# A decode kernel's TensorE program as loops of two units with fixed addresses: K turned into one of two slots, V landing in one of two, w_o between the loops

## The chip, the cores and the metric

The kernel runs on one core of one Trainium2 chip. The metric is device time in microseconds (us). Five engines work side by side, each from its own program: TensorE (PE), VectorE (DVE), ScalarE (ACT), GpSimd (POOL) and SyncE (SP), which here only issues transfers. Sixteen DMA engines carry the transfers.

## The reference, cut to what matters

Two layers of attention over a cache and a small feed-forward network, for 4 rows of 512 numbers, each layer run with the same weights and the same caches:

```python
for layer in range(2):
    x = x + attention(layernorm(x), k_cache, v_cache, wq, wo)
    x = x + (silu(n @ w_gate) * (n @ w_up)) @ w_down      # n = layernorm(x)
# attention: q = n @ wq, 32 heads; head h of row b reads group h // 4:
#   p = softmax(q . k_cache[b, g] / sqrt(128)), o = p @ v_cache[b, g], then o @ wo
# k_cache, v_cache: (4, 8, 8192, 128) bf16
```

There are 4 x 8 = 32 pairs of row and group. A pair is called a unit; it needs one K block and one V block of 8192 x 128 bf16, 2 MB each.

## The kernel before, in words

**Slots.** SBUF holds eight slots of 2 MB (`kv`, L157 to L158). `pump` (L316) walks one list of loads (`items`, L279 to L284) in order and issues the next whenever a slot fits: any free slot will do for any K or V, except that the last loads ahead of the feed-forward weights use slots 0 to 5 alone. The order of a layer is K0 K1 V0 K2 V1 K3 V2 ... and at its end w_gate, w_up and w_down, which take slots 6 and 7 and a piece behind them. Layer 1 starts with units 29, 30, 31, whose K and V are kept in six slots from layer 0 (L267 to L278); then come units 0 to 28. While they are worked through, V of unit 0 and K of unit 2 come in by halves over K of units 29 and 30 (`halves`, L288 and `half`, L350).

**One unit.** DVE turns K in place, in eight pieces q of 1024 keys (`turn`, L396, a 32 x 32 block transpose, L401). For each piece TensorE runs four score matmuls (`scores`, L414, L421) into one of two PSUM banks, so 32 a unit. The left-hand matrix `zq` holds the unit's queries between zeros; POOL writes it for each unit (L412). Then come the softmax steps: a maximum over the free axis (L427), a transpose (L431), a maximum of it (L434), a copy (L437), a spread by matmul (L443), exp on ACT (L449), a transpose on DVE (L454), the sum (L457, L459). For V, sixteen matmuls (`block`, L517) use the transposed p; ACT and DVE pick out and add the diagonal blocks (L526, L531), a matmul adds rows (L536), and DVE scales into `oT` (L556). The last two units of a layer do V in 64 small matmuls (L549). Once the four units of a group are done, `out_proj` (L575) multiplies by that group's part of w_o: 16 matmuls at L581, a DVE copy at L584, 16 matmuls at L587, and an addition to x.

**Order.** The program of every engine is written out flat. `keys` (L473) and `values` (L496) put blocks into a list with an estimated time each; `drain` (L467) emits them so that DVE's turning runs 2.0 us of estimated time ahead of TensorE; `advance` and `flush` (L382, L389) put the softmax steps (`line`) and the steps after V (`after`) between the blocks. TensorE takes V of unit u right after the scores of unit u+1: K0, K1, V0, K2, V1, K3, V2 and so on. `_Sync` (L21) keeps a count for each engine and puts in the waits. `finished` (L363) frees a slot behind the last matmul that reads it, and calls `pump`.

**Feed-forward.** `ffn` (L647) uses slots 6 and 7 for weights; at its end (L683) these two are free again, and K of units 0 and 1 of the next layer are loaded into them.

Of the kernel before, what the change touches and what calls it, by code (L numbers as in the profile page):

```python
# [6 lines left out]
ALU = mybir.AluOpType  # L7
# [13 lines left out]
class _Sync:  # L21

    def __init__(self, engines, prog_sems):
        self.eng = engines
        self.prog = prog_sems
        self.count = {n: 0 for n in engines}
        self.waited = {}
        self.res = {}
        self.semval = {}

# [24 lines left out]
    def _wait(self, engname, need):  # L55
        e = self.eng[engname]
        for sem, val in need:
            k = (engname, id(sem))
            if self.waited.get(k, 0) >= val:
                continue  # L60
            if sem is self.prog.get(engname) and (val > self.count[engname] or engname == "pe"):
                continue
            e.wait_ge(sem, val)
            self.waited[k] = val

    def _record(self, engname, sv, reads, writes):
# [6 lines left out]
        for r in reads:  # L73
            rec = self.res.get(r)
            if rec is None:
                rec = self.res[r] = _Rec()
            rec.r[engname] = sv

# [25 lines left out]
def bass_interleave_layers__gqa_block_cached__swiglu_ffn__decode_kernel(  # L104
# [43 lines left out]
    with ExitStack() as es:  # L148
# [7 lines left out]
        o4 = sb("o4", [P, REP, B], BF16)  # L156
# [24 lines left out]
        xs = sb("xs", [P, B], FP32)  # L181
        vs = sb("vs", [P, B], FP32)
        lnv = sb("lnv", [P, B], FP32)
        rstd = sb("rstd", [P, B], FP32)
        oT = sb("oT", [P, 2, REP, B], BF16)
# [4 lines left out]
        zq = sb("zq", [P, 4, ZP + P], BF16)  # L190
# [99 lines left out]
        free = list(range(NSLOT))  # L290
        slot_of = {}

# [23 lines left out]
        def pump():  # L316
            while issued[0] < len(items):
                n = issued[0]
                it = items[n]
                if it[0][0] == "w":  # L320
                    if it[0] == "wg":
                        if not {NKEEP, NKEEP + 1} <= set(free):
                            return
                        free[:] = [s for s in free if s < NKEEP]
                    load_weight(*it)
                    issued[0] += 1
                    continue

                late = any(e - 10 < n < e for e in ends)
                fit = [s for s in free if s < NKEEP or not late]  # L330
                if not fit:
                    return
                s = fit[0] if late else max(fit, key=lambda s: s >= NKEEP)
# [29 lines left out]
        def finished(it):  # L363
            kind, L, u = it
            if (kind, 1, u) in kept and L == 0:
                slot_of[kind, 1, u] = slot_of[it]
                if kind == "K":
                    turned.update((1, u, q) for q in range(NB))
            elif it in halves:
                half(it, 1)  # L370
                pump()
            else:
                free.append(slot_of[it])
# [22 lines left out]
        def turn(L, u, q):  # L396


            s = slot_of["K", L, u]
            w = kv[:, s, q * TB * Dh:(q + 1) * TB * Dh].bitcast(FP32)  # L400
            T.op("dve", lambda e: e.transpose(w, w), reads=[f"s{s}.{q}"], writes=[f"s{s}.{q}"])  # L401
            turned.add((L, u, q))

        def place_q(u, eng="pool", src=qr, keys_=SCR):
# [4 lines left out]
            dst = zq[:, :, ZP:].rearrange("p c (a x) -> p c a x", a=NA)[:, :, :, 0:REP]  # L409
# [4 lines left out]
        def scores(L, u, q):  # L414

            s = slot_of["K", L, u]
# [3 lines left out]
            for c in range(4):  # L420
                T.op("pe", lambda e: e.matmul(bank(bk)[:, 0:SW], lhsT=zq[:, c, z0:z0 + P], rhs=w[:, :, c // 2, :, c % 2],  # L421
                                              start=(q == 0 and c == 0), stop=(q == NB - 1 and c == 3)),
                     reads=[f"s{s}.{q}", "zq"], writes=[f"pb{bk}"], sig=(c == 3))
# [6 lines left out]
        def max_t(u):  # L430
            T.op("pe", lambda e: e.matmul(bank(STEP)[0:1, 0:P], lhsT=mx[:], rhs=identf[:], is_transpose=True,  # L431
                                          start=True, stop=True),
                 reads=["mx", "ident"], writes=[f"pb{STEP}"])
# [7 lines left out]
        def exps(u):  # L441
            bk = SBK[turn_of[u]]
            T.op("pe", lambda e: e.matmul(bank(STEP)[:, 0:1], lhsT=mrow,  # L443
                                          rhs=onesf[0:1, :], start=True, stop=True),
                 reads=["pb", "onesf"], writes=[f"pb{STEP}"])
# [10 lines left out]
        def total(u):  # L456
            T.op("pe", lambda e: e.matmul(bank(TOT)[:, 0:REP], lhsT=ones, rhs=rsm[:], start=True, stop=True),  # L457
                 reads=["rsm", "onesf"], writes=[f"pb{TOT}"])
# [4 lines left out]

        blocks = []
# [8 lines left out]
        def keys(L, u):  # L473
            def block(q):
                first = u == unit_order[L][0]
                if q == 0 and not first:
# [6 lines left out]
                if q == NB - 1:  # L483
                    finished(("K", L, u))
# [8 lines left out]

        done = set()

        def values(L, u):  # L496
            g, b = unit_gb(u)
            bk = OBK[turn_of[u]]

# [8 lines left out]
            def block(i):  # L508
# [5 lines left out]
                for t in range(TB):  # L514
                    j = t % NA
                    c0 = t * QB + i * NV * REP
                    T.op("pe", lambda e: e.matmul(bank(bk)[j * QB:j * QB + NV * REP, :],  # L517
                                                  lhsT=pT[:, turn_of[u], c0:c0 + NV * REP], rhs=v[:, t, NV * i:NV * (i + 1), :],
                                                  start=(i == 0 and t == j), stop=(i == 1 and t >= TB - NA)),
                         reads=[f"s{s}.{NV * i + k}" for k in range(NV)] + [f"pT{turn_of[u]}"], writes=[f"pb{bk}"],  # L520
                         sig=(t == TB - 1))
# [13 lines left out]
            def add_rows():  # L535
                T.op("pe", lambda e: e.matmul(bank(LNB)[:, 0:REP], lhsT=acc[:], rhs=head[:], start=True, stop=True),  # L536
                     reads=["acc", "head"], writes=[f"pb{LNB}"])
                scale_o(LNB)

            def block_last(q):  # L540
# [6 lines left out]
                for t in range(q * TB, (q + 1) * TB):  # L547
                    c0 = (t % TB) * QB + REP * q
                    T.op("pe", lambda e: e.matmul(bank(bk)[:, 0:REP], lhsT=kv[:, s, t * Dh:(t + 1) * Dh],  # L549
                                                  rhs=pT[:, turn_of[u], c0:c0 + REP], start=(t == 0), stop=(t == TT - 1)),  # L550
                         reads=[f"s{s}.{q}", f"pT{turn_of[u]}"], writes=[f"pb{bk}"], sig=(t % TB == TB - 1))
# [3 lines left out]
            def scale_o(k):  # L555
                T.op("dve", lambda e: e.tensor_tensor(oT[:, g // (G - 1), :, b], bank(k)[:, 0:REP], rl[:, rl_of[u], :],  # L556
                                                      ALU.mult),
                     reads=[f"pb{k}", f"rl{rl_of[u]}"], writes=[f"oT{g // (G - 1)}"])
# [8 lines left out]
            if all((L, g * B + k) in done for k in range(B)):  # L567
                rest.append([0.5, None, lambda: out_proj(g)])
# [6 lines left out]
        def out_proj(g):  # L575

            pick = ident.rearrange("p (j e) -> p e j", e=REP)
            ob = bank(OUTB)[:, XB:2 * XB].rearrange("p (e b) -> p e b", b=B)
            for c in range(REP):
                for h in range(REP):  # L580
                    T.op("pe", lambda e: e.matmul(ob[h * QB:(h + 1) * QB, c, :], lhsT=pick[:, c, :],  # L581
                                                  rhs=oT[:, g // (G - 1), h, :], start=True, stop=True),
                         reads=[f"oT{g // (G - 1)}", "ident"], writes=[f"pb{OUTB}"], sig=(h == REP - 1))
            T.op("dve", lambda e: e.tensor_copy(o4[:], ob), reads=[f"pb{OUTB}"], writes=["o4"])  # L584
            for nt in range(KT):
                for c in range(REP):
                    T.op("pe", lambda e: e.matmul(bank(OUTB)[:, nt * B:(nt + 1) * B],  # L587
                                                  lhsT=wo_sb[:, g, c, nt * P:(nt + 1) * P], rhs=o4[:, c, :],
                                                  start=(c == 0), stop=(c == REP - 1)),
                         reads=[f"wo{g // (G // 4)}", "o4"], writes=[f"pb{OUTB}"], sig=(c == REP - 1))  # L590
# [6 lines left out]
        def center():  # L597
            T.op("dve", lambda e: e.tensor_reduce(xs[:], xT[:].rearrange("p (k b) -> p b k", b=B), AX.X, ALU.add),
                 reads=["x"], writes=["xs"])
            T.op("pe", lambda e: e.matmul(bank(LNB)[:, 0:B], lhsT=ones, rhs=xs[:], start=True, stop=True),  # L600
                 reads=["xs", "onesf"], writes=[f"pb{LNB}"])
# [11 lines left out]
        def deviation(bias, bkey):  # L613
            T.op("pe", lambda e: e.matmul(bank(TOT)[:, 0:B], lhsT=ones, rhs=vs[:], start=True, stop=True),
                 reads=["vs", "onesf"], writes=[f"pb{TOT}"])
            T.op("act", lambda e: e.activation(lnv[:], bank(TOT)[:, 0:B], ACTF.Ln, scale=1.0 / D, bias=eps_sb[:]),
                 reads=[f"pb{TOT}", "eps"], writes=["lnv"])
            T.op("act", lambda e: e.activation(rstd[:], lnv[:], ACTF.Exp, scale=-0.5, bias=bias[:]),
                 reads=["lnv", bkey], writes=["rstd"])

        def qproj(gs, u=None):
            h0, nh = gs[0] * REP, len(gs) * REP
            for h in range(h0, h0 + nh):
                for kt in range(KT):
                    T.op("pe", lambda e: e.matmul(bank(LNB)[:, h * B:(h + 1) * B],  # L625
                                                  lhsT=wq_sb[:, kt, h * Dh:(h + 1) * Dh],
                                                  rhs=xn[:, kt * B:(kt + 1) * B],
                                                  start=(kt == 0), stop=(kt == KT - 1)),
# [7 lines left out]
            for c in range(4):  # L636
                for a in range(NA):
                    T.op("pe", lambda e: e.matmul(ob[a * QB:(a + 1) * QB, c, :, h0:h0 + nh],
                                                  lhsT=pick[:, c // 2, :, c % 2],
                                                  rhs=qT[:, :, h0:h0 + nh], start=True, stop=True),  # L640
# [120 lines left out]
```

## Time and profile before

| what | value |
|---|---|
| median of 3 runs | 654.95 us (654.82 to 656.93) |
| the profiled execution: its time | 655.51 us |
| its span, first to last instruction | 653.7 us |
| TensorE matmul busy | 500.5 us, 77% |
| DVE busy | 446.1 us, 68% |
| ACT, POOL busy | 18%, 3% |
| moved by DMA | 274.64 MB, 420 GB/s over the span |
| K loads: median from issue to landing | 30.0 us |
| V loads: median from issue to landing | 33.8 us |
| granted TensorE clock | 0.824 |

The page cuts the span into 40 slices of 16.3 us, and gives for each the busy share of each engine, the granted TensorE clock, the share of the DMA engines and the rate. It lists the DMA queues by kind: `hardware_dynamic` is the data, `instruction` is the fetching of programs (queue 8 in 16 KB packets, 38 of them; queue 14 in smaller ones). The trace keeps each DMA packet with its start and length, and for each load sixteen increments of its semaphore, one from each DMA engine, with their times: the first and the last tell when the earliest and the latest engine had its share of a load done.

### The profile page before, as it was taken

The numbers are of one execution on the slowest core, as the hardware profiler recorded it, in microseconds if no ns is written. First come the engines' busy times: TensorE is split into PE (matmuls) and PEld (weight loads), VectorE is DVE, ScalarE is ACT, GpSimd is POOL, SyncE is SP. The second block draws the span as 40 slices with busy tenths as digits, with TensorE's granted clock in tenths as the row PEclk, the third lists the DMA queues.
The fourth block names the chain that finished last, engine by engine and source line by source line (L and its number), as shares of the span: only waits on it lengthen the run. The fifth ranks groups of instructions, "written<-read, shape, count | busy, mean of one in ns | idle before, by whom it ended". The sixth has DMA issues, their size and how long they took to land.

```text
span 653.7 us, 11807 instructions
## 1 busy us (share of the span) xinstructions
PE 500.5 (77%) x4896; PEld 319.2 (49%) x4896; DVE 446.1 (68%) x1079; ACT 116.4 (18%) x391; POOL 19.3 (3%) x73
## 2 busy tenths in 40 slices
PE   1766787977777877787876988887688787786886
PEld 1544444544444544544555655554354454443456
DVE  2556676776776777776752399996677677676682
ACT  0021121221221221221220212221122122121120
POOL 0000000000000000000000000000000000000000
PEclk9897788777978778789685989997978887797895
DMA  9999999999999999999999999999999999999996
GB/s 368 428 425 423 438 429 427 432 431 429 430 431 429 430 430 432 430 432 428 427 416 375 398 411 431 430 428 429 430 428 429 433 430 430 432 427 429 432 420 239
DMA packets 24085, 274.64 MB, mean 420 GB/s; under 512 B 2392, under 2 KB 2400, under 8 KB 7904
## 3 DMA queue, kind: packets, MB, share of 16 engines
q1 hardware_dynamic: 24032, 273.89, 98.9%
q8 instruction: 38, 0.62, 0.3%
q14 instruction: 15, 0.12, 0.0%
HBM read 273.88 MB, written 0.00 MB: 419 GB/s over the span
## 4 chain that ended last, share of the span: by engine, by line
DMA 66%; DVE 17%; PE 13%; SPq 3%; issue 1%; ACT 0%; POOL 0%; DVEq 0%; POOLq 0%
DMA kvf<-in_A_k_cache_dram 63%; DVE kvf L401 11%; PE ps L421 8%; DVE acc L531 3%; DMA kvf<-in_B_w_down_dram 3%; SPq L93 2%; PE ps L517 1%; DVE one L427 1%; DVE pT L454 1%; PE ps L587 1%; DVE m L434 1%; PE ps L625 1%; PE ps L457 0%; PE ps L676 0%; PE ps L549 0%
## 5 line engine op out<-in xcount | busy, mean ns | idle before, releaser
L401 DVE STREAM_TRANSPOSE kvf<-kvf 128x512 f32<-128x512 f32 x488 | 322.4, 686 | 121.8 <-DMA kvf<-in_A_k_cache_dram 121.8
L421 PE MATMUL ps<-kvf,zq 128*128 128x256 bf16 x2048 | 346.2, 314 | 18.2 <-DVE kvf L401 15.7
L421 PEld LDWEIGHTS ps<-kvf,zq 128*128 128x128 bf16 x2048 | 211.3, 115 | 89.8 <-DVE kvf L401 40.4
L437 ACT ACTIVATE pb<-m 1x128 f32<-1x128 f32 x64 | 19.7, 308 | 453.5 <-DVE m L434 453.5
L431 PE MATMUL ps<-identf,one 128*1 128x128 f32 x64 | 18.3, 286 | 68.3 <-DVE one L427 68.3
L517 PE MATMUL ps<-kvf,pT 128*16 128x512 bf16 x960 | 68.5, 409 | 0.9 <-DVE rl L459 0.9
L531 DVE SCALAR_TENSOR_TENSOR acc<-ps,own,acc 128x128 f32<-128x128 f32 x180 | 63.1, 351 | 6.5 <-ACT acc L526 1.9
L431 PEld LDWEIGHTS ps<-identf,one 128*1 128x1 f32 x64 | 5.1, 80 | 99.4 <-DVE one L427 93.2
L536 PE MATMUL ps<-head,acc 128*128 128x4 f32 x120 | 26.4, 290 | 17.9 <-DVE acc L531 17.7
L536 PEld LDWEIGHTS ps<-head,acc 128*128 128x128 f32 x120 | 22.8, 237 | 34.2 <-DVE acc L531 33.6
L443 PE MATMUL ps<-one,pb 1*128 1x1 f32 x128 | 27.8, 284 | 14.1 <-ACT pb L437 13.8
L443 PEld LDWEIGHTS ps<-one,pb 1*128 1x128 f32 x128 | 22.4, 217 | 32.8 <-ACT pb L437 29.1
L449 ACT ACTIVATE pb<-ps,one,rstd 128x256 bf16<-128x256 f32 x64 | 36.2, 565 | 2.1
L412 POOL TENSOR_TENSOR zq<-scr,quad 128x64 bf16<-128x64 bf16 x62 | 18.2, 293 | 608.1 <-PE ps L421 569.4
L517 PEld LDWEIGHTS ps<-kvf,pT 128*16 128x16 bf16 x960 | 19.3, 91 | 32.8 <-issue 21.2
L427 DVE TENSOR_REDUCE one<-ps 128x1 f32<-128x256 f32 x64 | 25.6, 399 | 13.1 <-PE ps L421 12.7
L454 DVE STREAM_TRANSPOSE pT<-pb 128x256 bf16<-128x256 bf16 x64 | 25.9, 405 | 1.9 <-ACT pb L449 1.9
L457 PEld LDWEIGHTS ps<-rsm,one 128*128 128x128 f32 x128 | 24.5, 237 | 3.0 <-ACT rsm L451 0.9
L457 PE MATMUL ps<-rsm,one 128*128 128x4 f32 x128 | 21.6, 239 | 0.0
L447 ACT ACTIVATE one<-ps,rstd 128x1 f32<-128x1 f32 x64 | 16.7, 261 | 25.8 <-PE ps L443 25.8
L526 ACT ACTIVATE acc<-ps,own 128x128 f32<-128x128 f32 x60 | 20.6, 343 | 0.0
L434 DVE TENSOR_REDUCE m<-ps 1x4 f32<-1x128 f32 x64 | 15.6, 244 | 6.5 <-PE ps L431 6.5
(66 smaller groups left out, 165.9 us busy)
## 6 DMA issues: line engine op xcount, KB each, us to landing
kvf<-in_A_k_cache_dram SPq DMA_DIRECT2D x60, 2048.0 KB, 30.0
kvf<-in_A_v_cache_dram SPq DMA_DIRECT2D x58, 2048.0 KB, 33.8
wq_sb<-in_A_wq_dram SPq DMA_DIRECT2D x4, 1024.0 KB, 7.6
wo_sb<-in_A_wo_dram SPq DMA_DIRECT2D x4, 1024.0 KB, 34.5
kvf<-in_A_v_cache_dram SPq DMA_DIRECT2D x8, 512.0 KB, 19.3
kvf<-in_B_w_gate_dram SPq DMA_DIRECT2D x2, 1792.0 KB, 23.2
kvf<-in_B_w_down_dram SPq DMA_DIRECT2D x4, 768.0 KB, 16.0
kvf<-in_A_v_cache_dram SPq DMA_DIRECT2D x2, 1024.0 KB, 7.0
```

The costliest lines, as they stand in the source:

```text
L401: T.op("dve", lambda e: e.transpose(w, w), reads=[f"s{s}.{q}"], writes=[f"s{s}.{q}"])
L421: T.op("pe", lambda e: e.matmul(bank(bk)[:, 0:SW], lhsT=zq[:, c, z0:z0 + P], rhs=w[:, :, c // 2, :, c % 2], start=(q == 0 and c == 0), sto ...
L427: T.op("dve", lambda e: e.tensor_reduce(mx[:], bank(bk)[:, 0:SW], AX.X, ALU.max), reads=[f"pb{bk}"], writes=["mx"])
L431: T.op("pe", lambda e: e.matmul(bank(STEP)[0:1, 0:P], lhsT=mx[:], rhs=identf[:], is_transpose=True, start=True, stop=True), reads=["mx", " ...
L434: T.op("dve", lambda e: e.tensor_reduce(m4[:], bank(STEP)[0:1, 0:P].rearrange("p (x h) -> p h x", h=REP), AX.X, ALU.max, negate=True), rea ...
L443: T.op("pe", lambda e: e.matmul(bank(STEP)[:, 0:1], lhsT=mrow, rhs=onesf[0:1, :], start=True, stop=True), reads=["pb", "onesf"], writes=[f ...
L449: T.op("act", lambda e: e.activation(pb[:], bank(bk)[:, 0:SW], ACTF.Exp, bias=nm[:], scale=by, accum_out=rs[:]), reads=[f"pb{bk}", "nm", " ...
L454: T.op("dve", lambda e: e.transpose(pT[:, turn_of[u], :], pb[:]), reads=["pb"], writes=[f"pT{turn_of[u]}"])
L457: T.op("pe", lambda e: e.matmul(bank(TOT)[:, 0:REP], lhsT=ones, rhs=rsm[:], start=True, stop=True), reads=["rsm", "onesf"], writes=[f"pb{T ...
L517: T.op("pe", lambda e: e.matmul(bank(bk)[j * QB:j * QB + NV * REP, :], lhsT=pT[:, turn_of[u], c0:c0 + NV * REP], rhs=v[:, t, NV * i:NV * ( ...
L531: T.op("dve", lambda e: e.scalar_tensor_tensor(acc[:], bank(bk)[:, k * Dh:(k + 1) * Dh], own[:, k:k + 1], acc[:], op0=ALU.mult, op1=ALU.ad ...
L536: T.op("pe", lambda e: e.matmul(bank(LNB)[:, 0:REP], lhsT=acc[:], rhs=head[:], start=True, stop=True), reads=["acc", "head"], writes=[f"pb ...
```

## The change

**Slots have fixed uses.** For most units K lands in slot 0 to 3 (by u - 2, modulo 4) and DVE's turning writes it into slot 6 or 7 (by u modulo 2), where TensorE reads it; the landing slot is free once it is turned out. V lands in slot 4 or 5 (by u modulo 2). Units 0 and 1 land in 6 and 7 and are turned in place, and the units 29 to 31 and the last two of a layer are turned in place where they landed. `pump` still goes through the same list in order, but each load now has one slot, and the list waits for that one.

**TensorE's program is recorded first** (`T.pe` puts each matmul with its waits on a tape) and emitted at the end by `roll`. It looks for stretches in which unit n and unit n + 2 have the same instructions, addresses and semaphores, and the awaited values grow by a constant. Each such stretch of at least three repeats becomes a loop on TensorE of two units; at the head of each turn the awaited values are worked out in registers from the loop's counter. The loop's head is placed at the start of a fetch block. The other engines' programs stay flat.

**w_o.** `project` takes several groups at once, at four places between loops: at unit 14 and 26 of layer 0 (groups 0 to 2 and 3 to 5) and at positions 17 and 27 of layer 1 (groups 0 to 2 and 3, 4), with the copy on ACT; the other groups as before. `oT` has a place for each group.

Some small tensors share a place (`xs` and `lnv` become `vs`), and `zq` keeps one run of zeros instead of four.

```diff
-        free = list(range(NSLOT))
+        free = set(range(NSLOT))
+        NLAND = NSLOT - 4
+        scored = set()
+        def home(it):
+            kind, L, u = it
+            if kind == "K" and u < 2:
+                return NKEEP + u
+            if kind == "K" or it in split:
+                return (u - (2 if kind == "K" else 1)) % NLAND
+            return NLAND + u % 2
+        def turned_in(L, u):
+            if u < 2 or u >= NU - NRES or u in unit_order[L][-2:]:
+                return slot_of["K", L, u]
+            return NKEEP + u % 2
...
-                late = any(e - 10 < n < e for e in ends)
-                fit = [s for s in free if s < NKEEP or not late]
-                if not fit:
+                s = home(it)
+                if s not in free:
                     return
...
-            T.op("dve", lambda e: e.transpose(w, w), reads=[f"s{s}.{q}"], writes=[f"s{s}.{q}"])
+            T.op("dve", lambda e: e.transpose(dst, src), reads=[f"s{s}.{q}"], writes=[f"s{to}.{q}"])
             turned.add((L, u, q))
+            if q == NB - 1 and to != s:
+                free.add(s)
+                pump()
...
+        between = {(0, 14): [0, 1, 2], (0, 26): [3, 4, 5], (1, 17): [0, 1, 2], (1, 27): [3, 4]}
...
+        def roll():
+            ops = T.tape
+            part = [ops[a:b] for a, b in zip(heads, tails[1:] + [len(ops)])]
+            said = [[(repr(aps), [id(w[0]) for w in left], sig, kw) for aps, left, sig, kw in seg] for seg in part]
...
+            stops = [n for n in range(1, len(heads)) if heads[n] != tails[n] or n == NU] + [len(heads)]
...
+                    while m + 2 < stop and said[m] == said[m + 2] and strides(m) and strides(m) == strides(n + (m - n) % 2):
+                        m += 1
...
+                if turns < 3:
+                    continue
...
+                with nc.Fori(1, 1 + turns, 1, engines=(pe,), head_slot={pe: 0}) as i:
+                    value = {}
+                    for _, left, _, _ in body:
+                        for sem_, v in left:
+                            d, = step[id(sem_)]
+                            value[id(sem_), v] = nc.tensor.to_reg(i * d + (v - d))
+                    T.play(body, lambda sem_, v: value[id(sem_), v])
```

## The prediction

> **What bounds the kernel now.** I began with the slices of the page.
>
> ```profile
> PE   1766787977777877787876988887688787786886
> DVE  2556676776776777776752399996677677676682
> ```
>
> The slices of the transfers are steadier:
>
> ```profile
> DMA  9999999999999999999999999999999999999996
> GB/s 368 428 425 423 438 429 427 432 431 429 430 431 429 430 430 432 430 432 428 427 416 375 398 411 431 430 428 429 430 428 429 433 430 430 432 427 429 432 420 239
> ```
>
> The transfers run at 427 to 433 GB/s nearly all the time, and no engine is full except DVE in slices 24 to 27 (376 to 441 us). So the kernel ends when its bytes have been moved. There is one dip, slices 21 to 24 (327 to 392 us), between the layers.
>
> Next I read the queues.
>
> ```profile
> q1 hardware_dynamic: 24032, 273.89, 98.9%
> q8 instruction: 38, 0.62, 0.3%
> ```
>
> Queue 8 is TensorE's program: 38 packets of 16 KB. On average that is 0.3%, but a load is done only when the slowest of the 16 engines has done its share. In the packet records a data packet of 16 KB takes 611 ns; a fetch takes 879 to 968 ns and the data packet behind it 1.08 to 1.16 us, so each fetch holds up its DMA engine by 1.41 us. The lengths repeat with a period of eight (934, 932, 924, 967, 961, 954, 879, 878, then 942, 933, 924 ...), and where the packets can be followed one to the next, fetches eight apart lie on one engine: eight engines take turns, the other eight get none. The landing times show it: the first K has its first share at 17.3 and its last at 17.9 us, 0.6 apart; by 31.5 us the two are 1.9 apart, by 196 us 3.3, by 334 us 3.8. In the stages where the queue never runs dry it grows with fetches 1, 9, 25 and 33 (28, 181, 428 and 580 us). At the end it is 4.9 us (first engine 644.9, last 649.9).
>
> Then the chain of waits, for the dip:
>
> ```profile
> 333.72 17.27 DMA kvf<-in_B_w_down_dram
> 351.04 1.08 PE ps L676 x32
> 355.17 1.04 PE ps L421 x4
> ...
> 398.64 1.21 DVE kvf L401 x2
> ...
> 411.66 0.63 PE ps L421 x4
> 412.35 21.91 DMA kvf<-in_A_k_cache_dram
> ```
>
> From 352 to 412 us the chain is TensorE and DVE: six slots were kept, so little could be loaded ahead, and computation is behind. Last, the timeline of SP, with TensorE's V matmuls:
>
> ```profile
> 366.70 0.33 SPq L93 DMA_DIRECT2D kvf<-in_A_v_cache_dram  x1
> 371.77 0.33 SPq L93 DMA_DIRECT2D kvf<-in_A_k_cache_dram  x1
> 372.75 0.33 SPq L93 DMA_DIRECT2D kvf<-in_A_v_cache_dram  x1
> 384.17 0.33 SPq L93 DMA_DIRECT2D kvf<-in_A_k_cache_dram  x1
> 385.15 0.33 SPq L93 DMA_DIRECT2D kvf<-in_A_v_cache_dram  x1
> 398.11 1.04 PE L517 MATMUL ps<-kvf,pT 128*16 128x512 bf16 x16
> 399.24 0.36 SPq L93 DMA_DIRECT2D kvf<-in_A_v_cache_dram  x1
> ```
>
> These are layer 1's V1 (366.70), K3, V2, K4 (384.17) and V3 (385.15, in the slot that V31 left). V1 is worked through at 398.11 to 399.15, 20 us after it landed (378.9), and its slot is reloaded at 399.24.
>
> **The change, part by part.**
>
> *Fixed V slots: a new wait.* V3 may go into slot 5 alone, and slot 5 holds V1 until 399.2. SP's list is in order, so K5, V4 and all later loads queue behind V3. K4 (slot 2, free when V31 is done, 385.2) is then the last load under way; it lands first at about 392. From an idle queue, layer 1's K0 took from 349.02 to its first share at 355.88, 6.86 us, of which 4.87 is the load itself (the step from landing to landing); so 2.0 us pass ahead of the first byte. V3 lands first at 399.24 + 2.0 + 4.87 = 406.1 instead of 396.58: +9.5 us on an engine without fetches. Such an engine then goes without a gap to the end in both kernels (396.58 to 644.92 before), so this is never made up. Computation is not starved by it: V3 is needed at 412, K5 lands at 411.0 where DVE reaches it at 411.6; K6, at 420.7, is 1.2 late, and from there the transfers bound again.
>
> *The same wait elsewhere.* In steady state V u is done 4 to 8 us after landing, while K, V and K (14.6 us) are in the queue ahead of the load that needs its slot; less 2.0 that leaves some 5 us. The tightest are 242.72 + 2.0 against 246.1, when the earliest engine wants it, 1.4 us, and ahead of w_gate V30, which goes at 320.8 instead of 306.2 and is wanted at 323.9: 1.1 us. At the kernel's start V2 could go at 38.6 and is wanted at 46.6. I cost these at nothing; the cover is these margins, and where one is gone, each us over it is a us of the whole. K's four landing slots are freed by DVE, earlier than before, and slots 6 and 7 are rewritten a whole unit after TensorE read them: nothing.
>
> *Turning into another slot* (L401, 656 to 712 ns a piece in place): the trace shows no out-of-place one of this shape. Between -0.5 and +0.5 us for eight pieces, by that row's own width; one unit (K2) lies ahead of V1's end. I take 0.
>
> *The loop.* By the positions given for w_o, the stretches are 0 to 13, 14 to 25, 26 to 31, 32 to 48, 49 to 58 and 59 to 63, and six units at least must repeat: about 2 to 13, 14 to 25, 37 to 48 (ahead of it V0 and K0, K1 lie elsewhere) and 50 to 58, so some 44 of 64 units. A unit has 110 records of matmuls and weight loads (32 + 16 + 1 + 2 + 2 + 2 pairs), and fetches lie 250 records apart. Not streamed: 44 x 110 = 4840, less four bodies of some 270, less up to a block of padding for each: 12 to 13 blocks, so about 25 fetches instead of 38. By 350 us there were 19 and will be some 13: the engine hit most had three (1, 9, 17) and gets two, -1.4 us for the end of layer 0 and with it V1's end. After 401 us come about 10 instead of 15. The idle gap lets the engines start together, 0.6 to 1.3 apart (17.9 and 357.2 us), and one to two rounds add 1.4 to 2.8: a spread of 3.0 at the end instead of 4.9, -1.9 us.
>
> *Heads of turns.* About 30 awaited values, up to two register operations each. The trace has none on TensorE; the nearest row is its 82 semaphore instructions at 51 ns, so 0 (TensorE runs on what is queued) to 3.1 us a turn. By the table by stage TensorE is busy 158 of the 200 us from 100 to 300, so idle 4.1 us a turn: hidden, except in the catching-up stage, where the head of the third loop (K2) lies ahead of V1's end. There I take +0.5, near the low end: the V matmuls ahead of it (1.04 us) and the last score matmuls are still running while the head is worked out.
>
> *w_o between loops* is 64 matmuls for three groups where three times 32 stood; hidden in the same idle time. If that cover is gone, V's slots are freed later and the margins of 1.1 and 1.4 us are the first to go.
>
> Sum: 9.5 + 0.5 - 1.4 - 1.9 = +6.7 on the profiled 655.51, so 662.2; the median of the runs is 0.56 below that execution: 661.6 us.
>
> [...]
>
> **The rivals.**
> 1. *Fetches saved, nothing gained*: the slowest engine is not the one that sets the end, and both terms go. 655.0 + 10.0 = 665.0. Against it: steps of the spread at fetches 25 and 33. Chance 0.10.
> 2. *The loop is fetched anew in each turn*: the change doesn't do what it says. Two blocks and the next one for 22 turns are 66 fetches, 23 more flat: 89, eleven on each of eight engines. By 350 us six rounds instead of three (+4.2), after the gap a spread of 8 instead of 4.9 (+3.1), and the gap: 655.0 + 4.2 + 3.1 + 10 = 672. If only one block a turn is fetched, 665. For it: the trace shows fetches one block ahead, and no jump back. Against it: the period of eight looks like eight places of 16 KB. Chance 0.17. [...]
> 3. *Faster*: V1 is done in time. If V1 ended at 392 or before, the gap would close; what is left is 1.4 + 1.9 = 3.3 less: 651.6. All fetches gone would give 7.5 at most (3.2 and 4.3). It decides at V1's end near 393, 6 us sooner than now, where DVE at 4.9 of 5 us sets the pace: chance 0.08.
> 4. *Both about cancel* (V1 some 4 us sooner, or nearly no fetch left): 653 to 657. Chance 0.12.
>
> The forecast has 0.53, with its own range 658 to 665. A measurement of this kernel tells about 0.3%, 2 us, from no change. Faster: 0.08, same: 0.12, slower: 0.80. The range takes in the cancelling case and most of the refetching one: 653.5 to 672.
>
> **What would show it.** Right: between layer 1's K4 and V3 the landings step by 13 to 15 us instead of 4.9, V3's issue follows V1's last matmul, and one of the slices near 390 to 400 us falls well under 375 GB/s; queue 8 has 22 to 28 packets; the last load's spread is 2 to 4 us. Wrong: V3 issued before V1 is done; queue 8 with 38 packets or more, or one at each turn; other gaps between loads at the heads of turns.

## The result, and the profile after

The changed kernel takes 670.0 us (median of 6 runs, 669.44 to 670.9) against 655.29 us (6 runs) of the kernel before: ratio 1.0223, 95% interval 1.021 to 1.0236. It is 14.7 us slower; the forecast was 6.7. The profiled execution has a span of 668.2 us, 14.5 more than the one before. The queues first, then the slices of the transfers:

```profile
q1 hardware_dynamic: 24032, 273.89, 97.8%
q8 instruction: 24, 0.39, 0.2%
q14 instruction: 15, 0.12, 0.0%
```

```profile
DMA  8999999999999999999999968999999999999996
GB/s 364 427 423 421 430 425 428 427 430 424 427 428 426 424 432 428 425 423 430 417 397 351 411 276 324 428 425 429 430 428 421 426 431 429 425 426 429 424 417 247
```

TensorE's fetches fell from 38 to 24: the turns of a loop are not fetched again. Between the fetches at 42.0 and 169.2 us the first loop jumps back five times (62.6 to 143.9 us) and queue 8 has no packet. From one jump to the next the trace has 229 instructions of TensorE, fewer than the 250 that lie between two fetches of the flat program, so a turn that starts at a block's start fits into one block. Each of the five jumps takes 0.21 to 0.23 us; a branch of 2.7 us, with a fetch that starts within it, is seen further down, at a loop's entry.

There is a hole in slices 24 and 25 (384 to 418 us), as forecast. But the other slices are lower too: mostly 421 to 430 where 427 to 433 stood. The hole is where it was expected; SP's timeline, and V1's matmuls from TensorE's:

```profile
375.59 0.33 SPq L114 DMA_DIRECT2D kvf<-in_A_k_cache_dram  x1
376.57 0.33 SPq L114 DMA_DIRECT2D kvf<-in_A_v_cache_dram  x1
389.31 0.33 SPq L114 DMA_DIRECT2D kvf<-in_A_k_cache_dram  x1
402.26 1.04 PE L96 MATMUL ps<-kvf,pT 128*16 128x512 bf16 x16
403.39 0.33 SPq L114 DMA_DIRECT2D kvf<-in_A_v_cache_dram  x1
403.81 0.38 SPq L114 DMA_DIRECT2D kvf<-in_A_k_cache_dram  x1
```

These are K3, V2, K4 and, 14 us later and right behind V1's matmuls, V3, with K5 behind it. In the table by stage (busy us of PE, PEld, DVE, ACT, POOL, then clock, DMA share, GB/s) the hole is

```profile
390.00:395.00 5.00, 4.04 (x32) 2.65 (x31) 4.92 (x13) 1.77 (x6) 0.00 (x0) 1.00 0.95 344
395.00:400.00 5.00, 4.46 (x44) 2.63 (x43) 4.87 (x11) 1.77 (x6) 0.29 (x1) 1.00 0.25 102
400.00:405.00 5.00, 4.52 (x45) 2.57 (x44) 4.94 (x13) 0.58 (x3) 0.29 (x1) 1.00 0.24 46
405.00:410.00 5.00, 4.21 (x44) 2.53 (x42) 4.88 (x13) 1.19 (x4) 0.29 (x1) 1.00 0.91 374
```

DVE is busy 4.9 of 5 us all through: computation doesn't wait for the loads here, the loads wait for it. The landings step by 13.9 us from K4 to V3 (first shares at 396.2 and 410.1).

The rest of the loss is spread out. From V3's first share to the last load's first share it was 248.3 us; now it is 251.3, though the DMA engines never run dry (DMA share 1.01 from 412 to 640 us). In the packet records a 16 KB packet takes 614 (half of them), 621 or 613 ns where 611 stood, and the earliest engine steps from load to load in 4.90 us instead of 4.86, from the first K on, long before a loop or a second slot is used.

### The profile page after: what moved, and what is told of

The parts are those of the page before. It is cut to its first block, busy times and chain, and to the rows that moved or that the text cites. A ratio compares the mean times of both kernels' runs of the same rounds, so it can differ in the third digit from the quotient of the medians.

```text
span 668.2 us, 11716 instructions
## 1 busy us (share of the span) xinstructions
PE 495.3 (74%) x4784; PEld 320.2 (48%) x4784; DVE 443.3 (66%) x1061; ACT 116.8 (17%) x395; POOL 19.3 (3%) x73
## 4 chain that ended last, share of the span: by engine, by line
DMA 61%; PE 18%; DVE 14%; SPq 5%; issue 1%; ACT 0%; POOL 0%; DVEq 0%; POOLq 0%
DMA kvf<-in_A_k_cache_dram 56%; PE ps L96 18%; DVE kvf L435 9%; SPq L114 5%; DMA kvf<-in_B_w_down_dram 5%; DVE acc L573 2%; DVE one L464 1%; DVE pT L489 0%; DVE m L470 0%; ACT pb L473 0%; ACT acc L568 0%; DVE scr L688 0%; SPq L70 0%; DVE xT L613 0%; DVE oT L598 0%
## 5 line engine op out<-in xcount | busy, mean ns | idle before, releaser
L96 PE MATMUL ps<-kvf,pT 128*16 128x512 bf16 x960 | 65.1, 393 | 2.9 <-DVE rl L494 2.9
L96 PEld LDWEIGHTS ps<-one,pb 1*128 1x128 f32 x128 | 23.8, 230 | 29.5 <-ACT pb L473 20.1
L96 PE MATMUL ps<-one,pb 1*128 1x1 f32 x128 | 29.2, 295 | 10.8 <-ACT pb L473 10.8
L486 ACT ACTIVATE rsm<-head,one 128x4 f32<-128x4 f32 x64 | 19.0, 298 | 2.1
```

The lines of the kernel that those rows point to most:

```text
L96: ins = e.matmul(out, lhsT=lhsT, rhs=rhs, **kw)
L486: T.op("act", lambda e: e.activation(rsm[:], head[:], ACTF.Copy, scale=rs[:]), reads=["head", "rs"], writes=["rsm"])
```

## The experiments

Each kernel ran beside the kernel before on the same chip, and ratios are against it. Where two changed kernels are compared, the difference is that of their medians; the kernel before had medians of 655.1 to 655.3 us all along.

**First: which part of the change costs what.** Theory: two costs, the wait of V3, and one that lengthens every packet. The second had no cause yet. One part of the change that I had read over is where small tensors stand: `o4` (32 bytes) left its place ahead of the slots, and `vs` and `rstd` (16 bytes each, 32 reserved) came there. So all slots and weights start at 16672 instead of 16640.

*The changed kernel with the slots at 16640:*

```diff
-        rstd = sb("rstd", [P, B], FP32)
         kvf = sb("kvf", [P, NSLOT * SL + FR * F], BF16)
...
         identf = sb("identf", [P, P], FP32)
+        rstd = sb("rstd", [P, B], FP32)
```

> The changed kernel with one edit: the small tensor rstd stands behind the weights instead of ahead of the slots, so that the slots and all weights start 32 bytes lower, at 16640 (a multiple of 64) instead of 16672. Nothing else differs. Theory A (the address): a 32-byte shift makes every data packet longer (611 ns before, mostly 614 to 621 after), 0.9% of the transfer time; then packets of 611 ns come back, the earliest engine's step from load to load is 4.86 us instead of 4.90, and the time falls by 5 to 6 us, to 664 to 665. Theory B (the short queue): loads are slower because few of them are queued (15.8 us from issue to landing instead of 33.8), or because turning now writes a second slot; then the time stays at 670.

Measured: 663.05 us, ratio 1.012 (1.0103 to 1.0137), so 7.0 less than the changed kernel; packets of 611 ns. Theory A holds, B falls. The table by stage from 100 to 300 us, for the changed kernel and then for this one:

```profile
100.00:300.00 200.00, 149.67 (x1241) 93.66 (x1241) 140.38 (x324) 35.63 (x122) 5.85 (x20) 0.84 1.01 426
```

```profile
100.00:300.00 200.00, 151.73 (x1256) 94.75 (x1255) 141.03 (x325) 35.63 (x122) 6.16 (x21) 0.83 1.01 431
```

The DMA share is full in both; only the rate in the last column tells them apart.

*The kernel before with the slots at 16672:*

```diff
         o4 = sb("o4", [P, REP, B], BF16)
+        xs = sb("xs", [P, B], FP32)
...
-        xs = sb("xs", [P, B], FP32)
```

> The kernel before with one edit: the small tensor xs stands ahead of the slots, so that slots and weights start 32 bytes higher, at 16672 instead of 16640. Theory A (the address): packets of 614 to 621 ns, a step of 4.90 us, and 5 to 6 us more: 660 to 661. Theory B (short queue, second slot): 655.3, no change.

Measured: 661.67 us, ratio 1.0099 (1.008 to 1.0117): 6.4 more than before, by moving 16 bytes of unrelated data. Packets of mostly 614 to 621 ns.

*The kernel before with V3's wait alone:*

```diff
+                if it == ("V", 1, 3):
+                    fit = [s for s in fit if s == slot_of["V", 1, 1]]
                 if not fit:
                     return
```

> The kernel before with one edit: V of unit 3 in layer 1 may go only into the slot that V of unit 1 leaves; all else is as before. Theory (the new wait, as predicted): V3 is issued at 399.2 instead of 385.2, its first share lands near 406 instead of 396.6, +9.5 us that nothing makes up, less some 1 us because the gap lets the DMA engines start together again: 663 to 664.5. Rival (the gap is made up later, since loads wait anyway): 655 to 657.

Measured: 664.15 us, ratio 1.0142 (1.0122 to 1.0162): 8.9 more. One load of 130 waits, and nothing gives it back. V3 is issued at 399.88 and K5, V4, K6, V5 follow within 2.3 us, all of them held up:

```profile
384.80 0.33 SPq L93 DMA_DIRECT2D kvf<-in_A_k_cache_dram  x1
399.88 0.33 SPq L93 DMA_DIRECT2D kvf<-in_A_v_cache_dram  x1
400.26 0.42 SPq L93 DMA_DIRECT2D kvf<-in_A_k_cache_dram  x1
400.86 0.33 SPq L93 DMA_DIRECT2D kvf<-in_A_v_cache_dram  x1
401.28 0.80 SPq L93 DMA_DIRECT2D kvf<-in_A_k_cache_dram  x1
402.13 0.47 SPq L93 DMA_DIRECT2D kvf<-in_A_v_cache_dram  x1
```

*The changed kernel without that wait:*

```diff
+        early = {("K", 4): 6, ("K", 5): 7, ("V", 3): 2, ("V", 4): 3}
...
+            if L == 1 and it[0::2] in early:
+                return early[it[0::2]]
...
-            if u < 2 or u >= NU - NRES or u in unit_order[L][-2:]:
+            if u < 2 or u >= NU - NRES or u in unit_order[L][-2:] or (L == 1 and u < 4):
...
             elif kind == "K" and u < 2:
+                if L == 1:
+                    free.add(slot_of[it])
                 pump()
```

> The changed kernel with other places in layer 1 alone: K2 and K3 are turned in place, K4 and K5 land in slots 6 and 7 when K0 and K1 are done, V3 and V4 land in the slots of V31 and V0; from K6 and V5 on all is as changed, and TensorE's third loop starts some units later. Theory (the new wait): the hole ahead of V3 is gone, V3 lands first 9 us sooner, and the time falls by 8 to 9.5 us, to 660.5 to 662. Rival (the hole is only a part, the loop's heads are what costs in the catching-up stage): it falls by less than 5 us.

Measured: 661.98 us, ratio 1.0105 (1.0084 to 1.0126): 8.0 less, at the theory's edge. A smaller hole shows further on, 2.1 us ahead of V7, which waits for V5; the next run shows what makes V5 late.

**Second: do the two add up, and what is the loop worth?** Two edits together, then variants of that kernel, and one more address.

> The changed kernel with the edits of two earlier runs together: slots and weights start at 16640 again, and V3, V4, K4 and K5 of layer 1 do not wait (K2, K3 turned in place). Theory (two causes that add: the address and the wait): 670.0 less 7.0 less 8.0, so 655.0, within 1 us of the kernel before; the one hole left, some 2 us ahead of V7, eats what fewer fetches save. Rival (a third cost in the loop, hidden so far behind the two): 657 or more.

Measured: 655.23 us, ratio 1.0004 (0.999 to 1.0018). Taking away the two causes takes away the whole loss. What is left of the change costs and gains about the same. The hole of 2.1 us ahead of V7 is still there. In the chain of waits V7 is issued at 429.89 and K9 at 430.27, behind an idle TensorE:

```profile
418.19 1.79 PE ps L96 x21
419.98 2.89 issue
422.88 6.95 PE ps L96 x54
...
429.89 0.33 SPq L114
430.27 13.14 DMA kvf<-in_A_k_cache_dram
```

The 2.89 us are the entry of the third loop. Its branch takes 2.74 us, and a fetch of queue 8 starts 0.5 us into it; in the changed kernel the same branch takes 0.30 us (at 395.9), with a fetch 5.5 us ahead of it. That the branch waits for its block is inferred from these times. With the entry, V5 is worked through 10.0 us after V4 instead of 7.05. Without it V7 would have been issued near 426.9 and landed near 433.8 (an estimate, by the 2.0 + 4.87 us of an idle queue), before the 434.5 at which it is wanted: the entry makes the hole. The run before (V3 free, slots at 16672) has the same, a branch of 2.99 us with a fetch 0.6 us into it. So there is a third cost, of the loop itself, which the changed kernel, entering its third loop elsewhere, did not have. The gains against it are V3's first share 0.9 us sooner than in the kernel before and a last spread of 3.4 us instead of 4.9.

*V7 freed too* (`early` with K8 in slot 0, V7 in slot 2):

> As the run with both mended, and in layer 1 K8 lands in slot 0 and V7 in slot 2, so that V7 does not wait for V5. TensorE's third loop is gone by this (too few equal units), the others stand. Theory: the hole of 2 us ahead of V7 closes, some four more fetches add at most one round on part of the engines; 653 to 654.5, below the kernel before by 1 to 2 us. Rival (the loop's heads cost time): the loss of a loop helps too and it is below 652.5.

Measured: 655.38 us, ratio 1.0008 (0.9999 to 1.0017). Missed: there is a hole again. The third loop and its entry are gone, but K8 now waits until K6 is turned out of slot 0, issue at 425.2, again 2.1 us.

*The same as both mended, flat* (`if turns < 3` made `if turns < 99`, so no loop is formed):

> As the run with both mended, but TensorE's program is emitted flat, without any loop; addresses, slots and order are the same. It tells what the loop alone is worth. Theory (fetches hold up DMA engines): 36 or 37 fetches instead of some 26, the first and last engine 4 to 5 us apart at the end instead of 3, so 1.5 to 2.5 us more than with the loop. Rival 1 (VectorE's own program, fetched on one engine, sets the spread whatever TensorE does): no difference, under 0.5 us. Rival 2 (heads of turns cost time): faster than with the loop.

Measured: 655.66 us, ratio 1.0013 (1.0004 to 1.0023). 37 fetches instead of 26, the engines 3.8 apart at the end instead of 3.4. Loop and flat program differ by 0.4 us, and their intervals overlap: the theory's 1.5 to 2.5 us are not there. But the pair does not measure the fetches alone. The flat program has no entry to wait at: V5 follows V4 by 7.05 us, and the holes at V7 and K9 are 0.5 us together. With the loop the first share of K8 landed 1.9 us sooner (429.7 against 431.6), and V7's at the same time (436.6 against 436.8). The entry took back what stood ahead of it, so what fewer fetches are worth stays open.

*The kernel before, 64 bytes higher* (`xs` and `vs` ahead of the slots):

> The kernel before with two small tensors ahead of the slots, so that slots and weights start at 16704, 64 bytes higher than before, and 32 bytes higher than in the run that cost 6.4 us. If a packet is longer because its rows begin off a multiple of 64 bytes: packets of 611 ns and no change, 655.2. If it is longer because they begin off the place they had (a multiple of 256): 660 to 662 again.

Measured: 660.23 us, ratio 1.0086 (1.007 to 1.0101), 5.1 more. A multiple of 64 is not enough.

**Third: the step of the address, the last hole, and VectorE's fetches.**

*Eight units in the old order:*

```diff
+        early = {("K", 4): 6, ("K", 5): 7, ("V", 3): 2, ("V", 4): 3,
+                 ("K", 8): 6, ("K", 9): 7, ("V", 7): 2, ("V", 8): 3}
...
+            if u < 2 or u >= NU - NRES or u in unit_order[L][-2:] or (L == 1 and u in (2, 3, 6, 7)):
```

> As the run with both mended, and layer 1 keeps the old order of slots for longer: K6 and K7 are turned in place too, K8 and K9 land in slots 6 and 7, V7 and V8 in slots 2 and 3; fixed addresses from K10 and V9 on, so TensorE's third loop is gone and three stand. Theory: neither V7 nor K8 waits, the hole of 2.1 us in that place closes for good; 653 to 654, below the kernel before by 1 to 2 us. Rival: another hole takes its place or the spread at the end grows by as much; 655 to 656.

Measured: 654.03 us, ratio 0.9982 (0.9973 to 0.9991). The third loop is gone with its entry. No hole of over 0.5 us is left after 376 us, and this version is 1.1 us faster than the kernel before: at the cautious end of what was expected, and about the least that this measurement can tell. SP issues K and V in pairs 7 us apart again:

```profile
412.41 0.33 SPq L114 DMA_DIRECT2D kvf<-in_A_k_cache_dram  x1
413.40 0.33 SPq L114 DMA_DIRECT2D kvf<-in_A_v_cache_dram  x1
419.46 0.33 SPq L114 DMA_DIRECT2D kvf<-in_A_k_cache_dram  x1
420.44 0.33 SPq L114 DMA_DIRECT2D kvf<-in_A_v_cache_dram  x1
```

*The kernel before, 128 and 256 bytes higher:*

> The kernel before with four small tensors ahead of the slots: slots and weights start at 16768, 128 bytes higher than before, a multiple of 128 and not of 256. 32 and 64 bytes cost 6.4 and 5.1 us. If rows must begin on a multiple of 128: 655.2 and packets of 611 ns. If on a multiple of 256: 659 to 660.

> The kernel before with six small tensors ahead of the slots: slots and weights start at 16896, 256 bytes higher than before, a multiple of 512 (before, 16640 is a multiple of 256 and not of 512). If 256 is the step: 655.2, no change. If 512 is one and the kernel before stood off it: packets shorter than 611 ns and 650 or less. If the cost comes from moving the small tensors and not from the rows' addresses: about 660, as with 64.

Measured: 660.28 us, ratio 1.0076 (1.006 to 1.0091), and 655.28 us, ratio 0.9997 (0.9988 to 1.0007). So 256 bytes are the step among the five starts tried (655.1 to 655.3 us at 16640 and 16896, 660.2 to 661.7 at 16672, 16704 and 16768), 512 brings nothing more, and moving the small tensors is harmless in itself. Off the step most packets grew by 0.3 to 1.6% (613 to 621 over 611 ns; with 128 bytes a quarter stayed at 611), and the time by 0.8 to 1.0%. Why a packet takes longer there is not shown by these runs; nor is why 32 bytes cost more than 64 or 128.

*More program for VectorE:*

```diff
+            if (L == 0 and 4 <= u < 28) or (L == 1 and 10 <= u < 26):
+                for i in range(3):
+                    T.op("dve", lambda e: e.memset(dum[:, i:i + 1], 0.0), writes=[f"dum{i}"], sig=False)
             T.op("dve", lambda e: e.transpose(dst, src), ...
```

> As the run with both mended, with three tiny memsets of a tensor of their own (one column each) ahead of each turn in units 4 to 27 of layer 0 and 10 to 25 of layer 1, 960 more instructions for VectorE; TensorE's program is the same. They take some 1.4 us of VectorE a unit, which is idle 2.7 us a unit there. Theory (a program's fetch holds up a DMA engine, and VectorE's long ones all fall on the same engine): seven to eight more packets in queue 14, each 0.84 us on that engine, four in layer 0 and three in layer 1; the first and last engine 5 to 6 us apart at the end, and 5 to 6 us more: 660 to 661. Rival (what instruction fetches do to single engines does not reach the end): 655 to 656.

Measured: 662.56 us, ratio 1.0107 (1.0091 to 1.0122), 7.3 more than with both mended. Queue 14:

```profile
q14 instruction: 22, 0.18, 0.1%
```

Seven packets more. From 440 us on the spread of a load goes 0.6, 1.5, 2.3, 3.1, 4.0, 4.9, 5.7: a step of about 0.85 us at VectorE's fetches; as the steps add up, they fall on the same engine. The end of layer 0 comes 4.9 us later. The hole ahead of V7 grew by 1.9 us, about the part above the expected 5 to 6. The memsets do not explain that growth: VectorE has none from 380 to 455 us. The granted TensorE clock was lower there, 0.74 and 0.58 in the two stretches from 425 to 435 us, against 0.85 and 1.00 with both mended.

## Why the prediction failed in size, point by point

The direction and the main mechanism, the wait of V3, were right; the sum of +6.7 us lacked a term, the address of the slots. Against the profiled executions:

| step | forecast | changed kernel | with the slots at 16640 |
|---|---|---|---|
| V1's end, against 399.24 | -0.9 | +4.2 (403.4) | -0.2 (399.0) |
| V3's first share after V1's end (before: -2.7) | 6.9 | 6.7 | 6.8 |
| from there to the last load's first share | 248.3 | 251.3 | 248.7 |
| spread of the last load (before: 4.9) | 3.0 | 3.0 | 2.5 |
| span | +6.7 | +14.5 | +7.1 |

- **Fixed V slots, +9.5**: right. 9.4 by the rows of the changed kernel (V1's end to V3: from -2.7 to 6.7), 8.9 as the only edit in the kernel before, 8.0 when taken away from the changed one.
- **An engine without fetches "goes without a gap to the end in both kernels (396.58 to 644.92 before)"**: this is the step that failed. The prediction took that stretch, 248.3 us, to be the same in both kernels, and so put the address of the slots at nothing without a reason. There was no gap, but every packet was longer: +3.0 us on that stretch and, with the loads before it, 6.4 to 7.0 us in all. V1's end came 4.2 us later than before, and 4.4 us later than with the slots at 16640. The diff moves small tensors ahead of the slots; I had not asked what address that leaves for those behind them.
- **The loop**: 24 fetches where 25 were forecast, no fetch at a turn. The rival of a loop fetched anew falls. A body is 229 instructions and not 270, so it lies in one block, and the rival's two blocks a turn were too many. What the prediction did not have is a wait at a loop's entry, 2.9 us with both mended.
- **-1.9 for the spread at the end**: 4.9 to 3.0, right. **-1.4 at the end of layer 0**: with the slots in their place the last share of w_down came 0.9 us sooner (351.7 to 350.8). The term was oversized. I had counted TensorE's fetches alone; VectorE's, one each 78 us or so, cost 0.84 us each (309 ns, and 1.14 us for the packet behind) and, by the spreads that add up, all fall on one engine; at 319 us the spread was 3.5 instead of 3.75. The run with more program for VectorE shows that its fetches reach the end of the kernel. That they set a floor under what TensorE's can save is argued from it, and not shown: the flat program of the same slots is only 0.4 us away, but the loop's entry lies in between.
- **Heads of turns, +0.5**: not seen. TensorE sat 0.64 us at the third loop's entry (396.9) and 0.94 at the head of its third turn ("issue"), of which five register operations of 60 to 83 ns and a branch of some 208 ns can be seen in the trace. But the chain of waits from 395.32 to 401.72 us runs through VectorE, so the head at 396.9 delayed nothing. V1's end follows another event: the granted TensorE clock comes up from 0.5 to full at 358.4 us before, at 358.4 with the slots at 16640 and at 363.1 in the changed kernel, and V1 ends 40.7, 40.5 and 40.2 us later; over all fourteen profiles it is 39.9 to 40.7, with loops and without. In the kernel 256 bytes higher, with the program of the kernel before, the clock came up at 360.9 and V1 ended 1.6 us later than before. So terms of half a us at V1's end can't be told from one profile each.

```profile
396.90 0.79 PEld L96 LDWEIGHTS ps<-kvf,zq 128*128 128x128 bf16 x8 [0.64 <-issue]
...
427.92 1.20 PEld L96 LDWEIGHTS ps<-kvf,zq 128*128 128x128 bf16 x7 [0.94 <-issue]
```

- **The same wait elsewhere, nothing**: right up to K8. Ahead of V7 there were 2.1 us, seen once the large hole was mended and due to the entry of the third loop; in the changed kernel that loop starts sooner, at 395.9, and no such wait shows.
- **Turning into another slot, 0**: right, 686 ns a piece in both.
- **The rivals**: the cancelling case needed nearly no fetch left or V1 sooner; neither happened. The time of the case of refetched loops, 672, lies near the measured one, by chance: its mechanism did not occur. The case in which saved fetches gain nothing, 665.0, is not ruled out by time: with the slots at 16640 the kernel took 663.05, between it and the forecast of 661.6.
- **A reading of the slices**, "no engine is full except DVE": TensorE shows a 9 too, in slices 8 and 23. Nothing in the sum hangs on it.

Open: what the loop is worth where its entry does not wait, since no flat version of the kernel with eight units in the old order was run; why the branch at the third loop's entry took 2.7 to 3.0 us in three runs and 0.3 in the changed kernel; and which DMA engine a fetch falls on and why.

## What to carry to other kernels

In a kernel bound by transfers, two things decided here: that the queue never runs dry, and that each packet is as short as it can be (611 ns here, and mostly 613 to 621 with the slots at 16672). For the first, follow each load's slot to the last reader through every change of stage, not only in steady state: the depth that was enough while computation kept up failed here where computation was behind, at V3, and that cost 8.0 to 9.4 us. For the second, check the address of large buffers after any edit that moves a small one ahead of them, and put them on a multiple of 256 bytes: here 32, 64 and 128 bytes off it cost 5.1 to 6.4 us. When a program becomes a loop, look at the entry of the loop in the chain of waits (2.9 us with both mended), and not only at its turns.

## What the runs showed of the hardware that was not expected

- Rows of 16 KB that start 32, 64 or 128 bytes off a multiple of 256 cost 6.4, 5.1 and 5.1 us of 655; 256 bytes further cost nothing. The DMA share in the profile is full either way (1.01); only GB/s (426 or 427 against 430) and packet lengths show it.
- A fetch of program holds up the one DMA engine that carries it: 1.41 us for 16 KB of TensorE's, 0.84 us for 8 KB of VectorE's. TensorE's go round eight engines, VectorE's fall on one; the packet records don't name the engine, so this is inferred from lengths that repeat after eight (934, 932, 924, 967, 961, 954, 879, 878 ns, then 942, in the kernel before) and from spreads that add up (0.6 to 5.7 us in six steps with more program for VectorE). 960 more instructions on VectorE cost 7.3 us, of which some 2 were a hole.
- A loop of two units on TensorE, 229 instructions in the trace, ran up to six turns without a fetch at a turn; a head left TensorE idle for 0.6 to 1.0 us.
- The branch at the third loop's entry took 2.74, 2.99 and 2.87 us in three runs, each time with a fetch that started 0.5 to 0.6 us into it, and 0.30 us in the changed kernel, with a fetch 5.5 us ahead.
